# Tokens of experts 2 to 7 gathered as four row pieces and turned by VectorE in 32x32 blocks

## The chip, the cores and the metric

The kernel runs on one core of one Trainium2 chip. The metric is the device time of one execution in microseconds. Before the change it is 1288.38 us, the median of three runs (1286.62 to 1290.02).

## The reference

One transformer layer on 2048 tokens of width 448: layer norm, attention of 16 heads of width 28 that share one key and one value head, output projection and residual, then a second layer norm, a gate over 8 experts, and for each token the two experts with the highest gate values. In fp32:

```python
h = layernorm(x)
p = softmax(causal(q @ k.T * 28 ** -0.5))          # 16 query heads, one k/v head
x1 = x + (p @ v) @ wo
h2 = layernorm(x1)
gate = softmax(h2 @ w_gate)                         # 8 experts
w, idx = top_k(gate, 2)
y = sum(w[e] * (silu(h2 @ w1[e]) @ w2[e]) for e in idx)   # w1: 448x1792, w2: 1792x448
out = x1 + y
```

## The kernel before

The work has four stages on the profile's clock: projections (0 to 84 us), attention (84 to 626), a tail in which the last 512 tokens are normalised, gated and routed while expert 0 already works on two tiles (626 to 690), and the experts (690 to 1290).

**Two-part values.** Every fp32 operand of a product is split in a high and a low part, and a product is three: high by high, high by low, low by high. A token tile (128 tokens) is held transposed, as `xh` (4 blocks of 128 rows) and `xl` (3 blocks). The width of 448 is three and a half blocks; the fourth block holds the last 64 rows' high parts in its upper half and their low parts in its lower half, so the weights' last 64 rows are loaded twice (`load_dup`, L257 to L259, three transfers).

**Tokens on their way to an expert.** In attention, each chunk of 512 tokens ends with its normalised rows and its 8 gate values written to `xnd` in HBM (L407), one row of 456 values a token. Routing makes `il`, a 128 x 128 table of int32: column 16 e + t holds the 128 token rows of tile t of expert e. For a tile, GpSimd gathers 128 rows of `xnd` into one of three buffers (`gather`, L152), TensorE turns them in four transposes through the identity into a bank of PSUM (`transposes`, L242, called by `xprep`, L157), ScalarE writes the high parts (L233, L234), VectorE the low parts (L235, L236), and VectorE copies the expert's gate column (L163).

**An expert.** A run-time Switch on the token counts picks one of the arms written out for an expert: one or two groups of up to four whole tiles and a remainder. `mlp` goes through 14 steps, one for each 128 of the 1792 hidden columns. A step is `first` (11 products of the split w1 with all tokens of the group), ScalarE's two silu outputs (L1021, L1022), VectorE's low part (L1026), and `second` (three products a tile, adding to the tile's output in PSUM). TensorE goes on with the next step's `first` ahead of a step's `second`. At the group's end ScalarE and VectorE scale the outputs and GpSimd adds them into `out` by an indirect scatter (L1097).

**What is woven into the steps.** `hook(k)` runs at each step k. In an expert's first group `ready` prepares the weights of a later step: ScalarE rounds w1 and w2 (L140, L142), VectorE subtracts (L141, L143). `ahead` prepares the tokens that come next: in a last group the first four tiles of the next expert (gathers from step 3, one tile's transposes a step from step 9), before a second group that group's tiles (gathers from step 1, tiles from step 6). Each engine does what it is given in the order written; Switch arms, groups and steps set that order.

Of the kernel before, what the change touches and what calls it, by code (L numbers as in the profile page):

```python
# [37 lines left out]
NF = FF // 128  # L38
OFF = 512
ROW = D + E  # L40
SCALE = DH ** -0.5
BOUND = 30.0
LOOK = 1
# [6 lines left out]
def body(ctx, tc, x, wq, wk, wv, wo, wg, w1, w2, out):  # L50
# [22 lines left out]
    V.memset(ones, 1.0)  # L73

    xnd = dr.tile([OFF + S, ROW], F32, name="xnd")
    ild = dr.tile([128, 128], I32, name="ild")


    il = cst.tile([128, 128], I32, name="il")
# [9 lines left out]
    def const(v, shape):  # L89
# [2 lines left out]
            c = c.unsqueeze(1)  # L92
        return c.to_broadcast(list(shape))

    cw = cst.tile([128, 2 * E], I32, name="cw")
    tok = cst.tile([128, NT], F32, name="tok")
    pcol = cst.tile([128, 1], F32, name="pcol")
# [11 lines left out]
    G.memset(likely, 1)  # L109


    raws, slots, RAW, W = [], [], {}, {}

    def new_slots(pool, n):
        for _ in range(n):
# [41 lines left out]
    def xprep(pt, g, e, x2, i):  # L157
# [4 lines left out]
        weave(split_x(pt[:, :, 0:n], xh[:, :, sl], xl[:, :, sl]))  # L162
        V.tensor_copy(gt[:, i:i + 1], g[:, D + e:D + e + 1])  # L163

    ma = ctx.enter_context(tc.tile_pool(name="ma", bufs=1))
    new_raw(ma)
    new_raw(ma)
    new_slots(ma, 1)
    xa = [new_x(ma, "x0", 4)]
    gbuf = [ma.tile([128, ROW], F32, name=f"g{i}") for i in range(3)]  # L170
    il0 = ma.tile([128, 2], I32, name="il0")


# [77 lines left out]
    def keep_warm(o, n):  # L251

        for _ in range(n):
            mm(o, ident, ident, True, True)

    def load_dup(eng, dst, src):
        eng.dma_start(dst[:, 0:3], src[0:384].rearrange("(k p) n -> p k n", p=128))  # L257
        eng.dma_start(dst[0:64, 3], src[384:448])
        eng.dma_start(dst[64:128, 3], src[384:448])  # L259

    qd = [dr.tile([2, D, 512], F32, name=f"qd{c}") for c in range(NCH)]
    wgd = dr.tile([E, D], F32, name="wgd")
# [50 lines left out]
    def router(c, sm, L, pb, lo=0, n=4, sb4=None, x_out=None, pl=None, oneh=oneh):  # L313
# [381 lines left out]
    with ExitStack() as p2:  # L695
# [35 lines left out]
        def attention(general):  # L731
# [3 lines left out]
            def early(k):  # L735
                if k < 4:
                    V.tensor_copy(wos[k][0], hp3[:, k])
                    G.tensor_tensor(wos[k][1], hp3[:, k], f(wos[k][0]), op=ALU.subtract)
                elif k == 4:
                    pw = psm.tile([128, 512], F32, name="pm")  # L740
                    for k in range(4):
                        n = 128 if k < 3 else 64
                        PE.transpose(pw[0:E, k * 128:k * 128 + n], wgs[0:n, k], ident[0:n, 0:n])
                    V.tensor_copy(lb3[0:E, 0:D], pw[0:E, 0:D])
                    SP.dma_start(wgd[:, :], lb3[0:E, 0:D])
                elif k == 5:
                    SP.dma_start(wgb, wgd[None, :, :].to_broadcast([128, E, D]))
                elif k == 6:
                    for o_, n_ in ((xnd, ROW), (out, D)):
                        SP.dma_start(o_[0:OFF].rearrange("(r p) n -> p r n", p=128),  # L750
                                     xn3[:, 0:1, 0:n_].to_broadcast([128, OFF // 128, n_]))
                else:
                    load(k - 7)

# [241 lines left out]
    with ExitStack() as p3:  # L996
# [234 lines left out]
        def dve(*gens):  # L1231
# [8 lines left out]
                4.5: [(t_tr, 1), (prep, 9)], 4.75: [(prep, 8), (t_tr, 2), (t_gate, 0)],  # L1240
# [3 lines left out]
                8.75: [(prep, 10), dve((g_route, gates), (g_route, put, 1))], 9: [dve((g_route, put, 3)), (prep, 11)], 9.5: [(arms,)],  # L1244
# [30 lines left out]

        def pools(k):
            if k == NF - 1.5:
                rst.close()
                mc = p3.enter_context(tc.tile_pool(name="mc", bufs=1, side="right"))
                xs.append(new_x(mc, "x1", 4))  # L1280
                xb.extend(new_x(mc, "xb", 3.5))
                ybuf.extend(mc.tile([128, D], F32, name=f"y{i}") for i in (2, 3))
                xprep(bank(), gs[0], 0, xb, 0)
# [7 lines left out]
        def tiles(e, lo, n):  # L1291
            return [idx_of(e, lo + t) for t in range(n)]

        def ahead(k, e, lo, n, x2, G1, k0, k1):
# [15 lines left out]
        def run_groups(e, groups, weights, rests=False, begun=False):  # L1310
# [3 lines left out]
            for j, (n, t, x2) in enumerate(groups):  # L1314
# [3 lines left out]
                def hook(k):  # L1318
# [17 lines left out]
                        ready(e * NF + NF + 1)  # L1336
                    if not last:
                        n2, t2, x3 = groups[j + 1]
                        ahead(k, e, lo + n, max(n2 + (t2 > 0), 2), x3, G1, 1, 6)
                    elif e + 1 < E:  # L1340
                        ahead(k, e + 1, 0, 4, xs[(e + 1) % 2], G1, 3, 9)

                add_out(mlp(e, x2, n, t, tiles(e, lo, n + (t > 0)), hook, begun and j == 0))
                lo += n
# [2 lines left out]
        def rest(e, lo):  # L1347

            total = nc.values_load(cw[0:1, e:e + 1], min_val=lo + 1, max_val=16)
            with tc.For_i(lo, total, 2) as ti:  # L1350
                ix = hp.tile([128, 2], I32, name="ix", bufs=1)
                SP.dma_start(ix, ild[:, bass.ds(e * 16 + ti, 2)])
                gather.n = 0
                for i in range(2):
                    xprep(bank(), gather(ix[:, i:i + 1]), e, xb, i)
# [4 lines left out]

        for e in range(E):
            K = KINDS if e else KINDS0
            if e:
                if e + 1 < E:
                    kind.append(kind_of(e + 1))
# [38 lines left out]
_INS = ["A_x", "A_wq", "A_wk", "A_wv", "A_wo", "B_w_gate", "B_w1", "B_w2"]  # L1404


# [17 lines left out]
```

## Time and profile before

| what | value |
|---|---|
| time, median of 3 runs | 1288.38 us |
| the profiled execution: its time | 1292.12 us |
| its span | 1290.2 us |
| TensorE granted clock, mean | 0.99 |
| TensorE busy, projections (0 to 84 us) | 74.99 us |
| TensorE busy, attention (84 to 626) | 541.46 us |
| TensorE busy, tail (626 to 690) | 58.19 us |
| GpSimd gathers L152, count and mean | 42, 1033 ns |
| GpSimd scatters L1097, count and mean | 36, 1599 ns |

How to read it: PE is TensorE's products, PEld its weight loads (they run beside products), DVE is VectorE, ACT ScalarE, POOL GpSimd, SP SyncE, which issues most transfers. A row names the line, the engine, the operation, and output <- input. "x4" is a count of records. A group's row gives its busy time and the mean of one in ns. In brackets on a timeline stands the time that the engine was idle ahead of the row, and what ended it. A windows row has the window, its length, the busy time (and count) of PE, PEld, DVE, ACT and POOL, then the granted clock, the share of the DMA engines and GB/s.

### The profile page before, as it was taken

How to read it: one execution, taken by the hardware profiler on the slowest of the kernel's cores; microseconds unless marked ns; L12 is line 12 of the kernel's file. 1: busy time of each engine (PE TensorE's matmuls, PEld its weight loads, DVE VectorE, ACT ScalarE, POOL GpSimd, SP SyncE). 2: the span in 40 equal slices, each digit the busy share in tenths (PEclk: the TensorE clock that was granted, in tenths of full speed). 3: DMA queues.
4: the chain of work that ended last, by engine and by line, in shares of the span. 5: the costliest groups of instructions: out<-in, count | busy, mean ns of one | idle time of the engine just before them, and what ended most of it. 6: DMA issues, size and time to landing. Idle time of an engine off the chain costs nothing. (4 is left out here: it accounts for less than half of the span.)

```text
span 1290.2 us, 20993 instructions
## 1 busy us (share of the span) xinstructions
PE 1261.6 (98%) x7262; PEld 910.2 (71%) x7262; DVE 598.0 (46%) x1555; ACT 820.4 (64%) x1442; POOL 142.6 (11%) x181
## 2 busy tenths in 40 slices
PE   8999999999999999999999999999999999999996
PEld 7754444554455445545698888998899998898995
DVE  7623222474257723774573445524423454314463
ACT  5689999799988998898642444524423554323453
POOL 5211000000000000000211202102021120112020
PEclk8999999999999999999998999999999999999998
DMA  5732543323232323432363435605341654314462
GB/s 164 214 109 38 152 99 53 66 29 72 41 53 59 67 38 66 95 67 24 93 185 90 118 115 126 188 28 133 92 81 37 167 139 130 79 41 108 128 149 50
DMA packets 81860, 122.12 MB, mean 95 GB/s; under 512 B 10584, under 2 KB 68032, under 8 KB 81528
## 3 DMA queue, kind: packets, MB, share of 16 engines
q1 hardware_dynamic: 71720, 94.99, 30.6%
q0 software_dynamic: 9936, 24.85, 8.7%
q8 instruction: 74, 1.21, 0.4%
q14 instruction: 130, 1.06, 0.3%
HBM read 90.43 MB, written 24.25 MB: 89 GB/s over the span
## 5 line engine op out<-in xcount | busy, mean ns | idle before, releaser
L723 ACT ACTIVATE p<-s 128x1024 f32<-128x1024 f32 x382 | 364.8, 1043 | 0.5 <-issue 0.4
L1021 ACT ACTIVATE s<-p 128x256 f32<-128x256 f32 (+8 forms) x168 | 78.8, 469 | 362.8 <-PE p L62 223.0
L62 PE MATMUL y<-w2h,h 128*128 128x448 f32 (+2 forms) x952 | 281.8, 373 | 0.2 <-DVE h L1026 0.2
L62 PE MATMUL s<-qt,KT 114*128 114x512 f32 x1024 | 277.5, 411 | 1.7 <-ACT p L723 0.7
L62 PEld LDWEIGHTS s<-qt,KT 114*128 114x128 f32 x1024 | 184.6, 188 | 125.7 <-ACT p L723 64.0
L62 PE MATMUL acc<-p,vv 128*32 128x512 f32 x2036 | 245.3, 598 | 0.0
L1026 DVE TENSOR_TENSOR h<-s,h 128x256 fp32r<-128x256 f32 (+5 forms) x168 | 87.6, 521 | 322.7 <-ACT h L1022 306.6
L62 PEld LDWEIGHTS y<-w2h,h 128*128 128x128 f32 (+2 forms) x952 | 170.5, 187 | 18.7 <-DVE h L1026 0.6
L62 PE MATMUL y<-w2l,h 128*128 128x448 f32 (+3 forms) x504 | 177.9, 368 | 0.0
L719 ACT ACTIVATE p<-s 128x512 f32<-128x512 f32 x254 | 138.0, 596 | 48.0 <-PE s L62 39.5
L62 PEld LDWEIGHTS acc<-p,vv 128*32 128x32 f32 x2036 | 53.2, 109 | 106.7 <-issue 105.9
L152 POOL DMA_INDIRECT g<-xnd,il x42 | 43.4, 1033 | 702.5 <-DVE il L872 455.0
L62 PEld LDWEIGHTS y<-w2l,h 128*128 128x128 f32 (+3 forms) x504 | 91.1, 181 | 9.3
L813 DVE RECIPROCAL lb<-lb 128x128 f32<-128x128 f32 x60 | 56.8, 947 | 82.9 <-DMA lb<-o 82.9
L1097 POOL DMA_INDIRECT out<-y,il x36 | 57.6, 1599 | 294.3 <-DVE y L1089 257.9
L1022 ACT ACTIVATE h<-p 128x256 fp32r<-128x256 f32 (+8 forms) x168 | 77.8, 463 | 0.0
L141 DVE TENSOR_TENSOR w1l<-w1r,w1h 128x512 fp32r<-128x512 f32 x109 | 75.1, 689 | 4.1 <-ACT w1h L140 1.2
L140 ACT ACTIVATE w1h<-w1r 128x512 fp32r<-128x512 f32 x112 | 71.0, 634 | 2.2 <-issue 2.2
L143 DVE TENSOR_TENSOR w2l<-w2r,w2h 128x448 fp32r<-128x448 f32 x108 | 66.9, 620 | 0.0
L142 ACT ACTIVATE w2h<-w2r 128x448 fp32r<-128x448 f32 x112 | 64.8, 579 | 0.0
L852 DVE SCALAR_TENSOR_TENSOR junk<-xn,wgb 128x448 f32<-128x448 f32 x96 | 59.6, 621 | 2.6
L62 PE MATMUL p<-x1h,w1h 128*128 128x512 f32 (+2 forms) x224 | 55.3, 368 | 0.5 <-DVE y L1082 0.3
(323 smaller groups left out, 1437.4 us busy)
## 6 DMA issues: line engine op xcount, KB each, us to landing
w2r<-in_B_w SPq DMA_DIRECT2D x56, 448.0 KB
w1r<-in_B_w SPq DMA_DIRECT2D x56, 384.0 KB
qt<-qd SPq DMA_DIRECT2D x64, 224.0 KB
w1r<-in_B_w SPq DMA_DIRECT2D x112, 64.0 KB
qd<-w1r POOLq DMA_DIRECT2D x8, 504.0 KB, 7.2
lb<-o SPq DMA_DIRECT2D x60, 64.0 KB
xnd<-xn SPq DMA_DIRECT2D x4, 912.0 KB
xt<-in_A_x SPq DMA_DIRECT2D x3, 896.0 KB
```

The costliest lines, as they stand in the source:

```text
L62: return PE.matmul(o, a, b, start=start, stop=stop)
L140: A.activation(w[0], a, AF.Copy)
L141: yield eng.tensor_tensor(w[1], a, f(w[0]), op=ALU.subtract)
L142: A.activation(w[2], b, AF.Copy)
L143: yield eng2.tensor_tensor(w[3], b, f(w[2]), op=ALU.subtract)
L719: x = [A.activation(p[:, b], s[:, b], AF.Exp, scale=SCALE) for b in range(2)]
L723: A.activation(p, s, AF.Exp, scale=SCALE)
L852: V.scalar_tensor_tensor(junk, xn[:, 0:D], 1.0, wgb[:, e], op0=ALU.mult, op1=ALU.mult, accum_out=LG[c][:, i, e:e + 1])
L1021: A.activation(s[:, 0:n], p[:, 0:n], AF.Silu)
L1022: A.activation(h[:, 0:n], p[:, 0:n], AF.Silu)
L1026: V.tensor_tensor(h[:, 512:512 + n], s[:, 0:n], f(h[:, 0:n]), op=ALU.subtract)
L1097: d = G.indirect_dma_start(out=out[:, :], out_offset=bass.IndirectOffsetOnAxis(ap=idx, axis=0), in_=y, in_offset=None, compute_op=ALU.add)
```

## The change

For experts 2 to 7 a token is also stored as four rows of `xsd`, each with 128 plain fp32 values (columns 0, 128, 224 and 320 onward) and the 8 gate values. `pieces` and `piece_gates` write them, eight transfers on SyncE's queue behind each chunk's `xnd` (the last chunk's are in the `tail` table at 4.5 and 9.5); rows of zeros are written early, with those of `xnd`.

A tile is gathered by four indirect transfers (`gather4`): in transfer q, partition 32 j + i gets piece j of the tile's token 32 q + i. One VectorE instruction then transposes the tile's 32x32 blocks in place (`turn`); after it a partition holds one column of the tokens. `turned` writes high parts (ScalarE), low parts (VectorE), and forms the gate column by a masked sum over the four 32-partition quarters. The order in which columns come to lie on partitions differs from before, so the host orders the rows of w1 for experts 2 to 7 to suit, and appends the last 64 rows a second time; one transfer loads them in place of three.

`lists4`, at the start of expert 1, makes the lists for the four transfers out of `il`: sixteen products of a 32-column slice of the identity with `il` in fp32 on TensorE, one VectorE instruction (4 x row + piece), and one transfer to HBM. `plan` sets at which step of a group each tile is turned and split; the gathers are all issued from step 1. It counts 5 us of GpSimd for a tile's four gathers. For the arms that the token counts take, the steps (turn, split) are 5,6 6,7 7,8 9,10 in expert 1; 8,9 10,11 12,13 in expert 2's first group; 6,7 7,8 8,9 10,11 in expert 4 (384 columns); 5,6 6,7 7,8 9,10 in expert 6 (448 columns).

```diff
+    xsd = dr.tile([(OFF + S) * 4, SROW], F32, name="xsd")
...
-        load_dup(SP, a, w1[e][:, q * 256:(q + 1) * 256])
+        SP.dma_start(a, w1[e][:, q * 256:(q + 1) * 256].rearrange("(k p) n -> p k n", p=128))
...
+    def gather4(col):
+        st = stage[gather.n % len(stage)]
+        gather.n += 1
+        for q in range(4):
+            G.indirect_dma_start(out=st[:, q], out_offset=None, in_=xsd[:, :],
+                                 in_offset=bass.IndirectOffsetOnAxis(ap=col(q), axis=0))
+        return st
+
+    def turn(st):
+        v = st[:, :, 0:128].rearrange("p i (b r) -> p i b r", r=32)
+        V.transpose(v, v)
+
+    def turned(st, e, x2, i):
+        xh, xl, gt = x2
+        n = min(128, xh.shape[2] - i * 128) // 32
+        v = st[:, 0:n, 0:128].rearrange("p i (b r) -> p b i r", r=32)
+        hi, lo = (t[:, :, i * 128:i * 128 + 32 * n].rearrange("p b (i r) -> p b i r", r=32) for t in (xh, xl))
+        A.activation(hi[:, 0:3], v[:, 1:4], AF.Copy)
+        A.activation(hi[0:64, 3], v[0:64, 0], AF.Copy)
+        V.tensor_tensor(lo, v[:, 1:4], f(hi[:, 0:3]), op=ALU.subtract)
+        V.tensor_tensor(hi[64:128, 3], v[0:64, 0], f(hi[0:64, 3]), op=ALU.subtract)
+        V.scalar_tensor_tensor(own[:, 4:8], st[:, :, 128 + e], 1.0, own[:, 0:4], op0=ALU.mult, op1=ALU.mult,
+                               accum_out=gt[:, i:i + 1])
+
+    def pieces(xn, c):
+        rows = xsd[(OFF + c * 512) * 4:(OFF + c * 512 + 512) * 4].rearrange("(t p j) n -> p t j n", p=128, j=4)
+        for j, o in enumerate(FROM):
+            SP.dma_start(rows[:, :, j, 0:128], xn[:, :, o:o + 128])
...
                 SP.dma_start(xnd[OFF + c * 512:OFF + (c + 1) * 512, :].rearrange("(t p) n -> p t n", p=128), xn)
+                pieces(xn, c)
+                piece_gates(xn, c)
...
+        def lists4():
+            p = bank()
+            for q in range(4):
+                for j in range(4):
+                    mm(p[32 * j:32 * j + 32, q], ident[:, 32 * q:32 * q + 32], ilf, True, True)
+            V.scalar_tensor_tensor(il4[0], p, 4.0, quad[:, None, :].to_broadcast([128, 4, 128]), op0=ALU.mult, op1=ALU.add)
+            SP.dma_start(ild4[:, :, :], il4[0])
...
+            if e > 1:
+                if k == 1:
+                    gather.n = 0
+                    G1.extend(gather4(col4(e, lo + i)) for i in range(min(n, 3)))
+                for i in range(n):
+                    if k == P[i][0]:
+                        turn(G1[i])
+                    if k == P[i][1]:
+                        turned(G1[i], e, x2, i)
+                        if i + 3 < n:
+                            G1.append(gather4(col4(e, lo + i + 3)))
+                return
```

How the order of instructions moves, at two places. On VectorE, in expert 2's first group, a row before is one tile's split between two steps' weights and low parts (`w1l`, `w2l` are the weights' low parts, `h` the hidden layer's, `xbl`, `xbh` and `xbg` the next group's tokens and gates):

```order
L1026 TENSOR_TENSOR h_11932<-s_11930,h_11932 128x256
L1228 ISA x3
L141 TENSOR_TENSOR w1l_11879<-w1r_103,w1h_11878 128x512
L143 TENSOR_TENSOR w2l_11881<-w2r_104,w2h_11880 128x448
L235 TENSOR_TENSOR xbl<-pt,xbh 128x3x128
L236 TENSOR_TENSOR xbh<-pt,xbh 64x128
L163 COPY xbg<-g_114 128x1
L1026 TENSOR_TENSOR h_11933<-s_11931,h_11933 128x256
```

And after, at the first tile's turn (`gb` is the tile that holds all gather buffers):

```order
L1072 TENSOR_TENSOR h_11985<-s_11983,h_11985 128x256
L152 TENSOR_TENSOR w1l_11940<-w1r_118,w1h_11939 128x512
L154 TENSOR_TENSOR w2l_11942<-w2r_119,w2h_11941 128x448
L187 STREAM_TRANSPOSE gb<-gb 128x4x128
L1072 TENSOR_TENSOR h_11986<-s_11984,h_11986 128x256
L152 TENSOR_TENSOR w1l_11944<-w1r_118,w1h_11943 128x512
L154 TENSOR_TENSOR w2l_11946<-w2r_119,w2h_11945 128x448
L197 TENSOR_TENSOR xbl<-gb,xbh 128x3x128
L198 TENSOR_TENSOR xbh<-gb,xbh 64x128
L199 SCALAR_TENSOR_TENSOR own,xbg<-gb,own 128x4
L1072 TENSOR_TENSOR h_11985<-s_11983,h_11985 128x256
```

The turn is a step of its own ahead of the split, which reads `gb` in SBUF where it read PSUM (`pt`), and the gate copy has become a sum. On TensorE, in the same group before, one step's `first`, a tile's transposes, and the start of `second`:

```order
L62 MATMUL p_11928<-x0h,w1h_11870 128x256 x4
L62 MATMUL p_11928<-x0h,w1l_11871 128x256 x4
L62 MATMUL p_11928<-x0l,w1h_11870 128x256 x3
L242 MATMUL pt<-ident,g_114 128x128 x3
L242 MATMUL pt<-ident,g_114 64x128
L62 MATMUL y_39314<-w2h_11868,h_11933 128x448 x2
L62 MATMUL y_39314<-w2l_11869,h_11933 128x448
```

After, the same place:

```order
L64 MATMUL p_11982<-x0h,w1h_11927 128x256 x4
L64 MATMUL p_11982<-x0h,w1l_11928 128x256 x4
L64 MATMUL p_11982<-x0l,w1h_11927 128x256 x3
L64 MATMUL y_38760<-w2h_11925,h_11985 128x448 x2
L64 MATMUL y_38760<-w2l_11926,h_11985 128x448
```

The transposes are gone from the arms of experts 2 to 7 (and from expert 1's, for expert 2's tiles), and nothing stands in their place.

More of the change, by code (lines that the diff above doesn't have):

```diff
@@ L40 @@
 ROW = D + E
+SROW = 128 + E
+FROM = (0, 128, 224, 320)
 SCALE = DH ** -0.5
@@ L75, in body @@
     xnd = dr.tile([OFF + S, ROW], F32, name="xnd")
+    xsd = dr.tile([(OFF + S) * 4, SROW], F32, name="xsd")
     ild = dr.tile([128, 128], I32, name="ild")
+    ild4 = dr.tile([128, 4, 128], I32, name="ild4")
     il = cst.tile([128, 128], I32, name="il")
@@ L93, in const @@
         return c.to_broadcast(list(shape))
+    quad = cst.tile([128, 1], F32, name="quad")
+    own = cst.tile([128, 8], F32, name="own")
+    G.memset(own, 0.0)
+    for j in range(4):
+        G.memset(quad[32 * j:32 * j + 32], float(j))
+        G.memset(own[32 * j:32 * j + 32, j:j + 1], 1.0)
     cw = cst.tile([128, 2 * E], I32, name="cw")
@@ L109, in body @@
     G.memset(likely, 1)
-    raws, slots, RAW, W = [], [], {}, {}
+    raws, slots, RAW, W, il4 = [], [], {}, {}, []
     def new_slots(pool, n):
@@ L163, in xprep, with piece_gates @@
         V.tensor_copy(gt[:, i:i + 1], g[:, D + e:D + e + 1])
+    def gather4(col):
[23 more added lines that the diff above has]
+            SP.dma_start(rows[:, :, j, 0:128], xn[:, :, o:o + 128])
+    def piece_gates(xn, c):
+        rows = xsd[(OFF + c * 512) * 4:(OFF + c * 512 + 512) * 4].rearrange("(t p j) n -> p t j n", p=128, j=4)
+        for j in range(4):
+            SP.dma_start(rows[:, :, j, 128:SROW], xn[:, :, D:ROW])
     ma = ctx.enter_context(tc.tile_pool(name="ma", bufs=1))
@@ L169, in body @@
     xa = [new_x(ma, "x0", 4)]
-    gbuf = [ma.tile([128, ROW], F32, name=f"g{i}") for i in range(3)]
+    gb = ma.tile([128, 12 * SROW], F32, name="gb")
+    gbuf = [gb[:, i * ROW:(i + 1) * ROW] for i in range(3)]
+    stage = [gb[:, i * 4 * SROW:(i + 1) * 4 * SROW].rearrange("p (i n) -> p i n", i=4) for i in range(3)]
     il0 = ma.tile([128, 2], I32, name="il0")
@@ L748, in early @@
                 elif k == 6:
-                    for o_, n_ in ((xnd, ROW), (out, D)):
-                        SP.dma_start(o_[0:OFF].rearrange("(r p) n -> p r n", p=128),
-                                     xn3[:, 0:1, 0:n_].to_broadcast([128, OFF // 128, n_]))
+                    for o_, r_, n_ in ((xnd, OFF, ROW), (out, OFF, D), (xsd, 4 * OFF, SROW)):
+                        SP.dma_start(o_[0:r_].rearrange("(r p) n -> p r n", p=128),
+                                     xn3[:, 0:1, 0:n_].to_broadcast([128, r_ // 128, n_]))
                 else:
@@ L1239, in body @@
                 3.75: [(t_norm, 3, A), (t_norm, 1, A), (t_tr, 0), (t_norm, 2, V), (t_base,)],
-                4.5: [(t_tr, 1), (prep, 9)], 4.75: [(prep, 8), (t_tr, 2), (t_gate, 0)],
+                4.5: [(t_tr, 1), (prep, 9), (pieces, xn3, 3)], 4.75: [(prep, 8), (t_tr, 2), (t_gate, 0)],
                 5: [(t_tr, 3), (t_gate, 1), (t_gate, 2), (t_gate, 3)], 5.5: [(prep, 6)],
@@ L1277, in pools @@
             if k == NF - 1.5:
+                V.tensor_copy(ilf, il)
                 rst.close()
@@ L1280, in pools @@
                 xs.append(new_x(mc, "x1", 4))
+                il4.append(mc.tile([128, 4, 128], I32, name="il4"))
                 xb.extend(new_x(mc, "xb", 3.5))
@@ L1292, in tiles, with col4, plan, ahead @@
             return [idx_of(e, lo + t) for t in range(n)]
-        def ahead(k, e, lo, n, x2, G1, k0, k1):
+        def lists4():
+            p = bank()
+            for q in range(4):
+                for j in range(4):
+                    mm(p[32 * j:32 * j + 32, q], ident[:, 32 * q:32 * q + 32], ilf, True, True)
+            V.scalar_tensor_tensor(il4[0], p, 4.0, quad[:, None, :].to_broadcast([128, 4, 128]), op0=ALU.mult, op1=ALU.add)
+            SP.dma_start(ild4[:, :, :], il4[0])
+        def col4(e, t):
+            return lambda q: il4[0][:, q, e * 16 + t:e * 16 + t + 1]
+        def plan(n, t, m, since):
+            N = n * 128 + t
+            tb = max(N, 256) * 11 * .00046 + (n * 3 + (3 if t > 64 else 2 if t else 0)) * .205
+            pool, P = since * 2.2 + 2, []
+            for i in range(m):
+                k = P[i - 3][1] if i > 2 else 1
+                pool = max(pool, k * tb + 2) + 5
+                P.append([max(-int(-(pool + 4) // tb), P[-1][0] + 1 if P else 0)])
+                P[-1].append(P[-1][0] + 1)
+            over = max(P[-1][1] - NF + 1, 0)
+            return [tuple(max(k - over, 1) for k in p) for p in P]
+        def ahead(k, e, lo, n, x2, G1, k0, k1, P=None):
+            if e > 1:
[10 more added lines that the diff above has]
+                return
             if k == k0:
@@ L1353, in rest @@
                 gather.n = 0
+                if e > 1:
+                    ix4 = hp.tile([128, 4, 2], I32, name="ix4", bufs=1)
+                    SP.dma_start(ix4, ild4[:, :, bass.ds(e * 16 + ti, 2)])
                 for i in range(2):
-                    xprep(bank(), gather(ix[:, i:i + 1]), e, xb, i)
+                    if e > 1:
+                        st = gather4(lambda q: ix4[:, q, i:i + 1])
+                        turn(st)
+                        turned(st, e, xb, i)
+                    else:
+                        xprep(bank(), gather(ix[:, i:i + 1]), e, xb, i)
                 add_out(mlp(e, xb, 2, 0, [ix[:, i:i + 1] for i in range(2)]))
@@ L1362, in body @@
             K = KINDS if e else KINDS0
+            if e == 1:
+                lists4()
             if e:
@@ L1404, with laid_out @@
 _INS = ["A_x", "A_wq", "A_wk", "A_wv", "A_wo", "B_w_gate", "B_w1", "B_w2"]
+def laid_out(inputs):
+    w1 = np.asarray(inputs["B_w1"])
+    tail = [FROM[j % 2] + r for j in range(4) for r in range(32)]
+    rows = [f + 32 * k + r for k in range(3) for f in (32, 160, 256, 352) for r in range(32)] + tail
+    own = list(range(D)) + list(range(384, D))
+    w1 = np.stack([w1[e][own if e < 2 else rows] for e in range(E)])
+    return {**inputs, "B_w1": w1}
 def kernel(**inputs):
```

12 lines of the change are left out of this document (5 added, 7 removed).

## The prediction

> **What bounds the kernel now.** I read the page's busy shares first, then the windows cut at the stages, then TensorE's rows of the experts' stage, one step after another. From the page, the windows, and two views that group rows (all transposes of gathered tiles; VectorE's groups between 690 and 1290 us, where a row is count | busy, mean ns):
>
> ```profile
> PE 1261.6 (98%) x7262; PEld 910.2 (71%) x7262; DVE 598.0 (46%) x1555; ACT 820.4 (64%) x1442; POOL 142.6 (11%) x181
> ...
> 690.00:1290.00 600.00, 586.98 (x3187) 529.84 (x3185) 258.63 (x548) 246.33 (x577) 92.65 (x94) 0.99 0.41 104
> ...
> L242 PE MATMUL pt<-ident,g x156: 270/272/302, 675.1 to 1231.1; 128*128 128x128 f32 x117, 128*64 128x128 f32 x39
> ...
> L235 DVE TENSOR_TENSOR x1l<-pt,x1h 128x384 fp32r<-128x384 f32 x16 | 8.9, 555 | 0.6
> L235 DVE TENSOR_TENSOR x0l<-pt,x0h 128x384 fp32r<-128x384 f32 x12 | 6.7, 556 | 0.0
> L235 DVE TENSOR_TENSOR xbl<-pt,xbh 128x384 fp32r<-128x384 f32 x9 | 5.0, 551 | 0.0
> ```
>
> TensorE is busy 98% of the span and 587.0 of the 600 us in which experts run; VectorE 258.6, ScalarE 246.3, GpSimd 92.7. So the time is what TensorE is given to do, and what leaves TensorE there leaves the time, unless another engine falls behind within a step. The transposes are 156, four a tile, so 39 tiles; 16 + 12 + 9 = 37 of those are finished after 690 us, of which 4 are expert 1's, left as they were. The change takes 33 tiles off TensorE.
>
> **What a tile's transposes cost TensorE.** A step is one 128-column slice of the hidden layer, and its first row is always the x0h by w1h group. Steps in the 448-column, the 384-column and the 256-column groups, TensorE's timeline (start, duration, then the idle time before it in brackets):
>
> ```profile
> 1209.17 0.98 PE L62 MATMUL p<-x0h,w1h 128*128 128x448 f32 x4
> 1213.64 0.99 PE L62 MATMUL p<-x0h,w1h 128*128 128x448 f32 x4
> 1215.91 0.60 PE L242 MATMUL pt<-ident,g 128*128 128x128 f32 x4
> 1218.57 0.98 PE L62 MATMUL p<-x0h,w1h 128*128 128x448 f32 x4
> ...
> 1024.88 0.86 PE L62 MATMUL p<-x0h,w1h 128*128 128x384 f32 x4
> 1028.67 0.86 PE L62 MATMUL p<-x0h,w1h 128*128 128x384 f32 x4
> 1030.61 0.60 PE L242 MATMUL pt<-ident,g 128*128 128x128 f32 x4
> 1032.87 0.86 PE L62 MATMUL p<-x0h,w1h 128*128 128x384 f32 x4
> ...
> 804.95 0.64 PE L62 MATMUL p<-x0h,w1h 128*128 128x256 f32 x4
> 807.50 0.64 PE L62 MATMUL p<-x0h,w1h 128*128 128x256 f32 x4
> 809.84 0.63 PE L242 MATMUL pt<-ident,g 128*128 128x128 f32 x4 [0.86 <-DMA g<-xnd,il]
> 811.52 0.66 PE L62 MATMUL p<-x0h,w1h 128*128 128x256 f32 x4
> 814.52 0.64 PE L62 MATMUL p<-x0h,w1h 128*128 128x256 f32 x4
> ```
>
> Without and with a tile, a step takes 4.47 and 4.93 us (448 columns), 3.79 and 4.20 (384), 2.55 and 3.00 (256, the last two rows): 0.46, 0.41 and 0.45. I take 0.44, not the records' 0.60, which overlap. 33 x 0.44 = 14.5 us. The 0.86 us in which TensorE waits for a gather goes too, since TensorE no longer waits for gathers there: 0.9. Nothing is late next by itself, because the step lengths without a tile are seen in the same group, with the same VectorE and ScalarE work in the steps around.
>
> [...]
>
> **What the change puts on TensorE: the lists.** At the start of expert 1, sixteen products of a 32-column slice of the identity with the list turn it into four lists; an fp32 product shows as two records, so 32 records of 128 columns. Nothing like it is in the trace; nearest are a group with 32-row weights, one-hot bf16 products of 128 columns, and the place where it stands:
>
> ```profile
> 586.16 1.92 PE L62 MATMUL acc<-p,vv 128*32 128x512 f32 x16
> ...
> 666.98 0.69 PE L62 MATMUL y<-y 128*128 128x128 bf16 x8
> ...
> 721.61 0.47 PE L62 MATMUL p<-x1h,w1h 128*128 128x512 f32 x1 [0.35 <-DVE y L1082]
> ```
>
> 32 x 0.12 = 3.8 us by the first (taken: 32-bit, 32 wide), 32 x 0.086 = 2.8 by the second, and as little as 1.4 if 128 columns cost a quarter of 512. TensorE waits 0.35 us for VectorE near there, which the products fill: +3.5, bounds +1.0 to +4.2.
>
> **What it puts on VectorE and ScalarE.** Per tile the 32x32 turn is new; hi copies, lo and tail subtracts remain with another source; the gate copy becomes a masked sum of 4 elements. The tight place is expert 2's first group (2 tiles, 2.55 us a step, weights prepared in each). VectorE's, then ScalarE's groups, by form:
>
> ```profile
> L141 DVE TENSOR_TENSOR w1l<-w1r,w1h 128x512 fp32r<-128x512 f32 x97 | 66.9, 689 | 2.9
> L143 DVE TENSOR_TENSOR w2l<-w2r,w2h 128x448 fp32r<-128x448 f32 x97 | 60.1, 620 | 0.0
> L1026 DVE TENSOR_TENSOR h<-s,h 128x256 fp32r<-128x256 f32 x54 | 23.0, 425 | 84.3 <-ACT h L1022 77.8 <-ACT s L1021 6.6
> ...
> L236 DVE TENSOR_TENSOR x1h<-pt,x1h 64x128 fp32r<-64x128 f32 x16 | 4.6, 284 | 0.5
> ...
> L140 ACT ACTIVATE w1h<-w1r 128x512 fp32r<-128x512 f32 x97 | 61.5, 634 | 0.0
> L142 ACT ACTIVATE w2h<-w2r 128x448 fp32r<-128x448 f32 x97 | 56.1, 579 | 0.0
> ...
> L1021 ACT ACTIVATE s<-p 128x256 f32<-128x256 f32 x26 | 10.0, 385 | 24.4 <-PE p L62 19.3 <-PE y L62 3.7 <-ACT w2h L142 1.4
> ...
> L233 ACT ACTIVATE x1h<-pt 128x384 fp32r<-128x384 f32 x16 | 7.9, 495 | 0.0
> L234 ACT ACTIVATE x1h<-pt 64x128 fp32r<-64x128 f32 x16 | 4.2, 265 | 0.0
> ```
>
> A step with a turn: 0.43 + 0.69 + 0.62 + turn. The turn is not in the trace; it moves 128x512 values, as the 0.69 us group does (taken), bounds 0.55 (128x384) to 1.4 (double): 2.43 us, under 2.55, or 3.1. The step after: 0.43 + 0.69 + 0.62 + 0.555 + 0.284 + the 4-element sum, an estimated 0.15 (half the 64x128 row) = 2.73 on VectorE and 2 x 0.385 + 0.634 + 0.579 + 0.495 + 0.265 = 2.74 on ScalarE, both 0.2 over the step. Three tiles: +0.5, bounds 0 to +2. In steps of 3.79 us and more the same sums fit with about 1 us to spare. The turn waits for its four gathers; behind it on VectorE stand the next weights' lows and h, for which TensorE's second layer waits. That cover is priced under the rivals.
>
> **What it puts on GpSimd.** Four gathers of 128 rows of 544 bytes for one of 1,824: 132 in place of 33. GpSimd's rows, and the issue row with the median time to landing:
>
> ```profile
> 803.00 1.18 POOL L152 DMA_INDIRECT g<-xnd,il  x1 [5.50 <-PE p L62]
> 804.48 0.98 POOL L152 DMA_INDIRECT g<-xnd,il  x1 [0.30 <-issue]
> 805.77 0.95 POOL L152 DMA_INDIRECT g<-xnd,il  x1 [0.30 <-issue]
> ...
> 832.08 1.62 POOL L1097 DMA_INDIRECT out<-y,il  x1 [25.36 <-DVE y L1089]
> ...
> 834.00 1.82 POOL L1097 DMA_INDIRECT out<-y,il  x1 [0.27 <-DMA out<-y,il]
> ...
> g<-xnd,il POOLq DMA_INDIRECT x42, 3.9
> ```
>
> Gathers start 1.29 us apart, with as many rows to describe as the new ones have, so twelve in a row take 15.5 us and the third tile has landed 19.4 us after step 1. Its turn stands at step 12 in expert 2's first group (11 x 2.55 = 28.1 us after step 1), at 8 in the 384-column one (7 x 3.79 = 26.5), at 7 in the 448-column one (6 x 4.47 = 26.8): 7 to 9 us to spare. Cost nothing, hidden behind TensorE's products.
>
> **What it puts on the queues.** In attention each 512-token chunk's normalised rows go out a second time, 1.05 MB in 512-byte packets and four transfers of 32-byte packets, on SyncE's queue behind xnd. SyncE's next transfers there, the window in which the last such xnd write moved, and VectorE's wait for those next transfers:
>
> ```profile
> 589.39 3.20 SPq L803 DMA_DIRECT2D lb<-o  x4
> ...
> 574.00:577.00 3.00, 3.00 (x26) 1.64 (x19) 2.90 (x12) 2.68 (x4) 0.00 (x0) 1.00 0.75 280
> ...
> 598.46 0.95 DVE L813 RECIPROCAL lb<-lb 128x128 f32<-128x128 f32 x1 [9.10 <-DMA lb<-o]
> ```
>
> The xnd write fills 3 us at 280 GB/s; the pieces are about 3.7 us more, to 581, and the queue's next work is issued at 589.4. Hidden, with 8 us to spare. For the last chunk the pieces stand among expert 0's weight loads, where a late load would delay TensorE: 0 to +3, I take +0.3. One weight load in place of three moves the same bytes: nothing.
>
> **Sum.** -14.5 - 0.9 + 3.5 + 0.5 + 0.3 = -11.1 us. The profiled execution took 1292.1 us (span 1290.2), 3.7 above the median of 1288.4; it becomes 1281.0, and the median 1277.3. With every bound on its good side: 33 x 0.46 = 15.2, + 0.9 - 1.0 = 15.1 less, 1273. All on the bad side: 33 x 0.41 = 13.5, - 4.2 - 2 - 3 = 4.3 less, 1284.
>
> **Rivals.** About 0.3%, 3.9 us, is what a measurement here can tell from no change.
>
> *GpSimd sets the pace* (slower). A turn that waits holds up VectorE, then TensorE. It decides where twelve gathers outlast the spare time. With pitch p the third tile is late by 12 x (p - 1.29) - 7 us in each of 9 groups; the gain is used up at 1.2 us a group, p = 1.97. At 2.1 it is 2.7 us a group, 24 in all, 13 over the gain: 1302. For it: the scatters above start 1.92 us apart; the new gathers write smaller rows into one tile; and the new lo subtract reads two SBUF operands while gathers run. Were each gather to wait out one such VectorE instruction (0.69), p would be 1.98, just at the point. Against it: the weights' lows above read two SBUF operands in every step already, and the gathers among them take 0.95 to 1.18. [...] Chance 0.12.
>
> *The written pieces hold up the queue* (about no change). If transfers of small packets ran at a quarter of the rate, about 15 us for 3.7, lb would come 3 us late at 598 and the last chunk's loads 8 us late: +11 in sum, 1288. For it: the 32-byte packets, not seen as writes here; against: the 8 us of room in attention. Chance 0.10.
>
> *The small costs all land on the bad side*: lists 4.2, the tight group +2, the tail +3: 1284, still just faster. It lies in the forecast's own spread; its part over 1284.5 gets 0.04.
>
> **How the numbers follow.** Forecast 0.74 (1273 to 1284), GpSimd 0.12, queue 0.10, small costs 0.04. Leaving out the GpSimd case and the far end of the queue's, the range is 1272 to 1288. Faster (under 1284.5): 0.74 and a little of the queue's, 0.76; same: 0.12; slower: 0.12.
>
> **What would show it.** Right: about 33 fewer groups of four transposes on TensorE, steps of 4.47, 3.79 and 2.55 us throughout, 32 records of some 0.12 us near 721, gathers still 1.3 us apart, a turn near 0.7 us with no wait for its gathers. Wrong: idle time before the turn put down to gathers of xsd, gathers 1.9 us or more apart, TensorE waiting for h after a turn, a wait for lb longer than 9.1 us, or steps of 2.55 grown to 3 in expert 2.

## The result and the profile after

The changed kernel takes 1303.2 us (median of four runs, 1300.2 to 1309.6) against 1288.6 for the kernel before: a ratio of 1.012, 95% interval 1.008 to 1.016. It is slower by about 15 us where 11 us less were forecast. The profiled execution took 1301.95 us, its span 1300.1.

From the page of the changed kernel, its view of VectorE's groups (the turn) and its view of TensorE's waits (total, times, longest):

```profile
PE 1253.7 (96%) x7162; PEld 900.1 (69%) x7162; DVE 618.0 (48%) x1623; ACT 822.1 (63%) x1442; POOL 240.2 (18%) x289
...
L181 POOL DMA_INDIRECT gb<-xsd,il x132 | 130.8, 991 | 124.5 <-issue 85.6
...
L187 DVE STREAM_TRANSPOSE gb<-gb 128x512 f32<-128x512 f32 x33 | 23.3, 705 | 0.5 <-DMA gb<-xsd,il 0.5
...
PE y L64 <- ACT h L1068: 9.6, 5, 5.2
PE y L64 <- ACT s L1067: 4.8, 2, 2.8
...
PE p L64 <- issue: 2.6, 5, 1.0
```

TensorE's records add up to 7.9 us less (1253.7 against 1261.6), yet the span is 9.9 us longer: TensorE is idle for 46.4 us in place of 28.6. The turn, 0.705 us each, waited only 0.5 us in all for its gathers. What TensorE waits for are ScalarE's silu outputs (`s`, `h`) and, oddly, nothing ("issue"), neither of which delayed a second-layer product in the profile of before.

The intended gain is there, step by step. TensorE's timeline of the changed kernel at the same places as shown of before: two ordinary steps of 448 columns in which tiles are now turned, one of 384, and the products that make the lists:

```profile
1225.13 0.96 PE L64 MATMUL p<-x0h,w1h 128*128 128x448 f32 x4
1229.56 0.97 PE L64 MATMUL p<-x0h,w1h 128*128 128x448 f32 x4
1233.99 0.97 PE L64 MATMUL p<-x0h,w1h 128*128 128x448 f32 x4
...
1042.13 0.86 PE L64 MATMUL p<-x0h,w1h 128*128 128x384 f32 x4
1045.86 0.86 PE L64 MATMUL p<-x0h,w1h 128*128 128x384 f32 x4
...
718.01 1.08 PE L64 MATMUL pt<-ilf,ident 128*32 128x128 f32 x32
```

A step with a tile is 4.43 us where it was 4.93, and 3.73 where it was 4.20. The 32 records of the lists take 1.08 us.

The loss stands elsewhere. The same timeline in expert 2's first group, whose steps take 2.51 us:

```profile
801.82 0.63 PE L64 MATMUL p<-x0h,w1h 128*128 128x256 f32 x4
804.33 0.63 PE L64 MATMUL p<-x0h,w1h 128*128 128x256 f32 x4
807.20 0.62 PE L64 MATMUL p<-x0h,w1h 128*128 128x256 f32 x4
813.13 1.06 PE L64 MATMUL p<-x0h,w1h 128*128 128x256 f32 x4
819.04 0.63 PE L64 MATMUL p<-x0h,w1h 128*128 128x256 f32 x4
```

Two steps take 5.9 us each. Such steps stand in six groups, always while gathers run: against the ordinary step of their group they lose 0.7 us in expert 1, 6.8 and 6.9 in expert 2's two groups, 6.9 in expert 3's second, 4.0 in expert 4, 4.1 in expert 5's second, 29 us together. What happens in one is plainest in expert 3's second group. GpSimd's, TensorE's and ScalarE's timelines of the changed kernel there (twelve gathers from 959.23 to 973.08, the first and the last shown):

```profile
959.23 1.04 POOL L181 DMA_INDIRECT gb<-xsd,il  x1 [0.30 <-issue]
960.57 0.98 POOL L181 DMA_INDIRECT gb<-xsd,il  x1 [0.30 <-issue]
...
971.83 0.94 POOL L181 DMA_INDIRECT gb<-xsd,il  x1 [0.30 <-issue]
973.08 0.95 POOL L181 DMA_INDIRECT gb<-xsd,il  x1 [0.30 <-issue]
...
968.11 0.60 PE L64 MATMUL p<-xbl,w1h 128*128 128x320 f32 x3
...
971.37 0.60 PE L64 MATMUL p<-xbl,w1h 128*128 128x320 f32 x3
977.19 1.20 PE L64 MATMUL y<-w2h,h 128*128 128x448 f32 x2 [5.22 <-ACT h L1068]
...
962.30 0.44 ACT L1067 ACTIVATE s<-p 128x320 f32<-128x320 f32 x1 [2.49 <-issue]
...
976.37 0.44 ACT L1067 ACTIVATE s<-p 128x320 f32<-128x320 f32 x1 [9.21 <-issue]
...
977.02 0.45 ACT L1067 ACTIVATE s<-p 128x320 f32<-128x320 f32 x1
```

TensorE ends two steps' first-layer products at 968.71 and 971.97. ScalarE, free since 967.15, starts their silus at 976.37 and 977.02: 7.7 and 5.1 us late, where 0.04 to 0.1 us is usual. Its wait at that point is for semaphores of VectorE and TensorE; VectorE's last work was done at 967.74. The trace's record of semaphore updates (the signals by which one engine tells another that work is done) settles which: after two at 971.34 and 971.38 a single one of TensorE's arrives, at 973.51, then eleven within 0.42 us from 976.30 on, some 3 us after the last gather began. The products behind those of 968.11 start at their usual distances, so the work was done and the news of it was late. I call the time from the end of a step's first-layer products to ScalarE's start the lag. Before, it is over 1 us in two steps of 138 after 725 us (1.06 at 807.5, in the only group whose three gathers meet steps this short, and 1.3 at the last scatters); after, in 17, at most 8.1. ScalarE's news is not late: VectorE, when it is free, starts on ScalarE's `h` 0.03 us after it as a rule and 0.09 at most, with gathers running or not.

Twelve gathers do not always cost time. In the longest steps (4.96 us: the first groups of experts 3 and 5) the lags are 0.7 and 2.8 us and TensorE loses nothing; in expert 6's group the first nine gathers stand 1.6 to 1.8 us apart, and the lag stays at 0.1.

The same backlog shows on TensorE itself, which stands still between products that have no wait (TensorE's timeline, expert 2's second group, gathers running since 837.6):

```profile
851.77 0.39 PE L64 MATMUL p<-xbl,w1h 128*128 128x288 f32 x1 [0.21 <-issue]
853.19 0.29 PE L64 MATMUL p<-xbl,w1h 128*128 128x288 f32 x1 [1.03 <-issue]
853.92 0.40 PE L64 MATMUL p<-xbl,w1h 128*128 128x288 f32 x1 [0.44 <-issue]
855.73 0.74 PE L64 MATMUL y<-w2h,h 128*128 128x448 f32 x1 [1.41 <-ACT h L1068]
```

A part of the loss is not idle time. Behind four of these stops TensorE's granted clock is half of full. Windows of the changed kernel, in and behind a stop of expert 2's second group, then of expert 3's:

```profile
849.90:853.90 4.00, 2.35 (x14) 1.86 (x12) 0.00 (x0) 0.00 (x0) 1.89 (x2) 0.99 0.20 52
853.90:860.70 6.80, 5.38 (x17) 4.23 (x17) 2.57 (x9) 2.04 (x6) 1.13 (x2) 0.50 0.00 1
...
972.70:976.70 4.00, 0.00 (x0) 0.00 (x0) 0.00 (x0) 0.33 (x1) 1.02 (x2) 1.00 0.13 35
976.70:980.10 3.40, 2.91 (x8) 2.37 (x9) 1.12 (x4) 1.09 (x4) 0.00 (x0) 0.51 0.00 0
```

With two more such stretches, at 812.9 and 1157.6, these are 17.1 us between 690 us and the last 10 us of the span, where the kernel before has none. The records stretch accordingly: two products of 0.57 us as a rule take 1.20 at 977.19.

### The profile page after: what moved, and what is told of

Same layout as the page of the kernel before. It is cut to its first block, busy times and chain, and to the rows that moved or that the text cites. A ratio compares the mean times of both kernels' runs of the same rounds, so it can differ in the third digit from the quotient of the medians.

```text
span 1300.1 us, 20906 instructions
## 1 busy us (share of the span) xinstructions
PE 1253.7 (96%) x7162; PEld 900.1 (69%) x7162; DVE 618.0 (48%) x1623; ACT 822.1 (63%) x1442; POOL 240.2 (18%) x289
## 3 DMA queue, kind: packets, MB, share of 16 engines
q14 instruction: 130, 1.06, 0.3%
## 5 line engine op out<-in xcount | busy, mean ns | idle before, releaser
L181 POOL DMA_INDIRECT gb<-xsd,il x132 | 130.8, 991 | 124.5 <-issue 85.6
L163 POOL DMA_INDIRECT gb<-xnd,il x9 | 9.9, 1098 | 502.3 <-DVE il L918 454.6
```

The lines of the kernel that those rows point to most:

```text
L181: G.indirect_dma_start(out=st[:, q], out_offset=None, in_=xsd[:, :], in_offset=bass.IndirectOffsetOnAxis(ap=col(q), axis=0))
```

## The experiments

The theory (A): gathers issued by GpSimd one right behind the other delay TensorE's semaphore updates; ScalarE starts late, then VectorE, then TensorE's second layer. The rivals (B): the new VectorE and ScalarE work, or the bytes of the gathers, hold up the steps; later, that GpSimd's being busy or the mere arrival of many small transfers does it.

| run | edit | median, us | ratio to before, 95% |
|---|---|---|---|
| e1_spaced | one small memset ahead of each gather | 1305.1 | 1.009 to 1.019 |
| e2_paced | gathers issued at later steps | 1303.6 | 1.008 to 1.015 |
| e3_before_extra | before, with three more gathers behind each | 1318.9 | 1.019 to 1.028 |
| e4_tiny | rows of 32 bytes | 1305.0 | 1.009 to 1.015 |
| e5_pool_work | iota in place of gathers | 1274.3 | 0.986 to 0.990 |
| e6_sp | SyncE's transfers in place of gathers | 1272.0 | 0.985 to 0.988 |
| e7_pitch | two longer memsets ahead of each gather | 1302.7 | 1.007 to 1.011 |
| e8_bursts | 4.7 us of memsets behind every four | 1294.8 | 1.003 to 1.005 |
| e9_bursts_planned | 2.3 us, and turns planned for it | 1276.2 | 0.988 to 0.991 |
| e10_short_planned | 1.2 us, and turns planned for it | 1276.6 | 0.989 to 0.992 |
| e11_plan_only | e9 without its memsets | 1316.1 | 1.019 to 1.023 |
| e12_half_rows | gathers of 64 rows | 1317.1 | 1.019 to 1.024 |

**e1_spaced.**

```diff
         for q in range(4):
+            G.memset(spacer, 0.0)
             G.indirect_dma_start(out=st[:, q], ...
```

> The changed kernel with one small GpSimd memset ahead of each of the four gathers, as the scatters have one between them; nothing else. Theory A: a run of gathers started 1.25 us apart delays TensorE's semaphore updates, ScalarE starts its silu up to 8 us late and TensorE stands still, 29 us in all. With a pitch of about 1.9 us the lag from the end of a step's first-layer products to ScalarE's start stays under 0.3 us, and the time falls from 1303 to about 1274; up to 1282 if the third tile, landed 12 x 1.9 + 4 = 27 us after step 1, comes too late for its turn in some groups. Theory B (the new VectorE and ScalarE work, or the bytes of the gathers, hold up the steps): 1300 to 1306, as the changed kernel.

1305.1 us, but the edit didn't do what it was meant to. Between the scatters the same memset takes 0.63 us; here 0.088, inside the 0.3 us that lie between gathers anyway, and the gathers stayed 1.25 us apart for the most part. The lags stayed too (up to 7.5 us). It tells nothing between the theories.

**e2_paced.**

```diff
...
-                if k == 1:
-                    gather.n = 0
-                    G1.extend(gather4(col4(e, lo + i)) for i in range(min(n, 3)))
+                for i in range(min(n, 3)):
+                    if k == P[i][2]:
+                        G1.append(gather4(col4(e, lo + i)))
```

> The changed kernel with the first three tiles' gathers issued not all at step 1 but two or three steps apart (at least 7.5 us from tile to tile where the group is long enough), turns planned after that; pitch within a tile's four gathers still 1.25 us. Theory A, if a backlog builds up only over a long run: lags under 0.3 us, 1274 us, range 1271 to 1280. If the pitch itself does it, four in a row also delay: a lag of about a microsecond a tile, 1285 or so. Theory B: 1300 to 1306.

1303.6 us, and again no pace: nothing ties a gather to a step. GpSimd goes on to the next gather whatever stands beside it in the program; the trace shows the same runs of twelve, 1.25 us apart for the most part, and lags up to 6.7 us. The edit paced nothing, so this too tells nothing between the theories.

**e3_before_extra.**

```diff
+        if more4:
+            for q in range(3):
+                G.indirect_dma_start(out=dump[(gather.n * 3 + q) % 5], out_offset=None, in_=xnd[:, :].rearrange("a b -> (a b)")[0:rows * 136].rearrange("(r n) -> r n", n=136),
+                                     in_offset=bass.IndirectOffsetOnAxis(ap=idx, axis=0))
         return g
...
```

> The kernel before, with three more gathers of 128 rows of 544 bytes behind each gather for experts 2 to 7, into buffers that nobody reads; TensorE still transposes. Theory A: the gathers alone bring the lags, TensorE loses 20 to 30 us, 1309 to 1320 (a few us of it waits of the transposes for gathers that now land later). Theory B: the extra gathers are hidden, 1287 to 1292.

1318.9 us, 30 us more than before. From its page (the 99 added gathers) and its view of TensorE's waits:

```profile
L156 POOL DMA_INDIRECT dump<-xnd,il x99 | 97.0, 980 | 31.7 <-issue 31.4
...
PE y L62 <- ACT h L1027: 17.0, 6, 5.5
PE pt L247 <- issue: 2.0, 2, 1.0
```

Nobody reads what these gathers bring, nothing else was changed, and the waits for ScalarE's `h` appear, with lags up to 10.8 us. That the new VectorE work is needed for the loss is out. The gathers alone cost 30 us, as much as the 29 us counted in the changed kernel.

**e4_tiny.**

```diff
-            G.indirect_dma_start(out=st[:, q], out_offset=None, in_=xsd[:, :],
+            G.indirect_dma_start(out=st[:, q, 128:SROW], out_offset=None, in_=xsd[:, :].rearrange("a b -> (a b)")[0:(OFF + S) * 4 * 8].rearrange("(r n) -> r n", n=8),
...
```

> The changed kernel with rows of 32 bytes in place of 544 in each gather (the tiles' 128 values are not brought, so the experts work on other data); as many gathers and rows as before. Theory A, with the number of row descriptors and not the bytes as the cause: lags as in the changed kernel, 1298 to 1306. If the bytes or the traffic are the cause: lags gone, 1272 to 1280.

1305.0 us: a seventeenth of the bytes, the same loss. Not the bytes.

**e5_pool_work.**

```diff
-            G.indirect_dma_start(out=st[:, q], out_offset=None, in_=xsd[:, :],
-                                 in_offset=bass.IndirectOffsetOnAxis(ap=col(q), axis=0))
+            for _ in range(3):
+                G.iota(st[:, q], pattern=[[1, SROW]], base=0, channel_multiplier=0, ...)
```

> The changed kernel with every one of the 132 gathers of experts 2 to 7 replaced by three iota instructions of GpSimd that write the same 136 columns (so these experts work on counted numbers): GpSimd is busy for as long, but describes no transfers. If describing or completing gathers delays TensorE's updates: no lag over 0.3 us but for the few in expert 0's stage, 1272 to 1278. If GpSimd's being busy (its port, its instructions) is the cause: lags as in the changed kernel, 1298 to 1306.

1274.3 us. GpSimd was busy for less than meant (396 iotas of 0.25 us are 94 us, against 131 of gathers), but after 725 us there is no lag over 0.9 us, and those over 0.3 stand at scatters. In e9_bursts_planned GpSimd is busy for 307 us in all (240 in the changed kernel), and the lag is gone as well. Being busy is not it.

**e6_sp.**

```diff
-            G.indirect_dma_start(out=st[:, q], out_offset=None, in_=xsd[:, :],
-                                 in_offset=bass.IndirectOffsetOnAxis(ap=col(q), axis=0))
+            SP.dma_start(st[:, q], xsd[OFF * 4 + q * 128:OFF * 4 + q * 128 + 128])
```

> The changed kernel with each gather replaced by a plain transfer of 128 rows of 544 bytes from the same table, issued by SyncE (so the tiles hold other tokens): as many transfers, rows, bytes and completions, described by hardware and not by GpSimd. If GpSimd's describing is the cause: no lags, 1272 to 1280 (a little more where a weight load stands behind a fourth tile's transfers on SyncE). If arrival and completion of many small transfers is the cause: lags as before, 1298 to 1306.

1272.0 us, 17 us under before. As many transfers with as many bytes, issued by SyncE and closer together (twelve in 7.8 us in expert 2's first group), and after 725 us no lag over 0.4 us but at scatters (1.7 at most). From its page and its view of VectorE's groups:

```profile
PE 1243.6 (98%) x7162; PEld 896.1 (71%) x7162; DVE 618.7 (49%) x1623; ACT 822.9 (65%) x1442; POOL 108.6 (9%) x157
...
L186 DVE STREAM_TRANSPOSE gb<-gb 128x512 f32<-128x512 f32 x33 | 23.3, 705 | 0.0
```

GpSimd has 132 records fewer than in the changed kernel (157 for 289). TensorE is back at 98% and 10.1 us less busy with the same products, and a turn that never waits hides wholly. This is what the change is worth without the lag, and the lag needs GpSimd's gathers.

**e7_pitch.**

```diff
         for q in range(4):
+            G.memset(wide, 0.0)
+            G.memset(wide, 0.0)
             G.indirect_dma_start(out=st[:, q], ...
```

> The changed kernel with two memsets of 300 values ahead of each gather, meant to set the gathers some 1.9 us apart (the 1-value memset of the earlier run took 0.09 us and left the pitch at 1.25). If the rate is the cause, as the stretch of expert 6 suggests, where gathers 1.6 to 1.8 us apart showed lags of 0.1 us: lags under 0.3 us, 1274, up to 1284 if third tiles land too late for their turns. If any long run of gathers is the cause, whatever its rate: 1300 to 1310.

1302.7 us, for another reason than the changed kernel. The gathers now stand 1.85 to 3.8 us apart, and ScalarE's `h` is gone from TensorE's waits. In its place, in VectorE's groups, TensorE's waits and ScalarE's timeline:

```profile
L190 DVE STREAM_TRANSPOSE gb<-gb 128x512 f32<-128x512 f32 x33 | 23.4, 709 | 66.6 <-DMA gb<-xsd,il 66.5
...
PE y L64 <- DVE h L1075: 20.9, 13, 3.7
...
826.40 0.52 ACT L198 ACTIVATE xbh<-gb 128x384 fp32r<-128x384 f32 x1 [4.36 <-DVE gb L190]
827.03 0.36 ACT L1070 ACTIVATE s<-p 128x256 f32<-128x256 f32 x1
```

The turns wait 66.5 us for gathers that come later, and VectorE's `h` behind them: the wait that was the prediction's GpSimd rival, here made by the cure. The longest lag left, 4.2 us, is ScalarE's own copy in front of the silu, which waits for a turn. The time lies in the range that was expected if any long run of gathers does the harm, but by accident. The trace's record of TensorE's updates settles the question: each of the 872 that add one after 725 us arrives within 0.22 us of the end of its product. So runs of up to sixteen gathers, 1.85 us or more apart, delay no update: it is the pitch that matters.

**e8_bursts.**

```diff
             G.indirect_dma_start(out=st[:, q], ...
...
+        for _ in range(12):
+            G.memset(wide, 0.0)
         return st
```

> The changed kernel with twelve memsets of 300 values behind each tile's four gathers, about 4 us of other GpSimd work between bursts of four gathers 1.25 us apart. If the backlog of TensorE's updates needs a run of more than four or five: lags under 0.5 us, 1274 to 1282. If it is the pitch within a burst: lags of 1 to 3 us remain, 1282 to 1300.

1294.8 us, in the range that was expected if the pitch within a burst did it, but again the rows show another cause. Four gathers 1.25 us apart and then a pause bring no lag of their own (all 872 such updates arrive within 0.02 us); the longest that is left, 3.9 us at 871, is ScalarE's copy behind a turn. The rest is the turn (46.7 us of waiting for gathers) and TensorE's 12.9 us for VectorE's `h`.

**e9_bursts_planned.**

```diff
+        for _ in range(6):
+            G.memset(wide, 0.0)
         return st
...
                 P[-1].append(P[-1][0] + 1)
-            over = max(P[-1][1] - NF + 1, 0)
-            return [tuple(max(k - over, 1) for k in p) for p in P]
+                pool += 2.5
+            last = [min(p[0], NF - 1 - m + i) for i, p in enumerate(P)]
+            return [(k, k + 1) for k in last]
```

> The changed kernel with six memsets of 300 values (some 2.4 us) behind each tile's four gathers, and turns planned for 7.5 us a tile in place of 5, none shifted earlier than its tile needs. In the run with twelve memsets ScalarE's lag was gone, but turns waited 46.7 us in sum for gathers that came later. If both are cured: ScalarE's lag under 0.5 us, turns waiting under 10 us in sum, 1276, range 1272 to 1283, so faster than the kernel before (1289). If 2.4 us between bursts is too short for the backlog: lags of 2 us and more return, 1285 to 1300.

1276.2 us, 12.6 under the 1288.8 of the kernel before in the same comparison. In every step that ends while gathers run, ScalarE starts within 0.1 us, and the turns wait 0.5 us in all: both waits are cured. (Two lags over 0.5 us are left, against what was expected, 2.3 us at 726 and 1.5 at 1229.5; both stand at scatters, with no gather of the split rows near.) Its timelines of GpSimd and ScalarE in expert 3's second group, and its groups of VectorE and waits of TensorE:

```profile
952.37 0.94 POOL L182 DMA_INDIRECT gb<-xsd,il  x1 [0.30 <-issue]
953.30 2.32 POOL L185 MEMSET wide<- 1x300 f32 x6
955.99 0.95 POOL L182 DMA_INDIRECT gb<-xsd,il  x1 [0.37 <-ACT h L1071]
...
958.05 0.44 ACT L1070 ACTIVATE s<-p 128x320 f32<-128x320 f32 x1 [2.46 <-issue]
...
961.30 0.44 ACT L1070 ACTIVATE s<-p 128x320 f32<-128x320 f32 x1 [2.49 <-issue]
...
L190 DVE STREAM_TRANSPOSE gb<-gb 128x512 f32<-128x512 f32 x33 | 23.3, 705 | 0.5 <-DMA gb<-xsd,il 0.3
...
PE y L64 <- DVE h L1075: 1.1, 2, 0.9
```

ScalarE comes every 3.25 us, as the 320-column steps do, through all the gathers.

**e10_short_planned.**

```diff
-        for _ in range(6):
+        for _ in range(3):
...
-                pool += 2.5
+                pool += 1.3
```

> The same with three memsets (some 1.2 us) behind each tile's four gathers and 6.3 us a tile in the plan. If a short pause lets TensorE's updates catch up: 1274 to 1282, as the run with six. If the mean rate of gathers decides (four in 6.3 us against four in 7.5 and twelve in 15): lags between those of the changed kernel and those of the longer pause, 1280 to 1295.

1276.6 us. A gap of 2.44 us in place of 1.25 from every fourth gather to the next is enough, though sixteen gathers then run within 23 us in expert 2's second group.

**e11_plan_only.**

```diff
-        for _ in range(6):
-            G.memset(wide, 0.0)
         return st
```

> The run with six memsets, its later turns kept and the memsets taken out. If the pause between bursts did it: lags of several microseconds are back and the time is 1295 to 1306, as the changed kernel. If the later turns did it: 1273 to 1280.

1316.1 us, above the range that was expected, with lags up to 10 us. So the pause cures the lag and the later turns do not. Why it is 13 us slower than the changed kernel is only known in part: its runs of gathers are the same length, but in its profile TensorE is idle for 57.6 us (46.4 in the changed kernel) and has the half clock for 41 us before the last stretch (17.1).

**e12_half_rows.**

```diff
-            G.indirect_dma_start(out=st[:, q], ...ap=col(q), axis=0))
+            G.indirect_dma_start(out=st[0:64, q], ...ap=col(q)[0:64], axis=0))
```

> The changed kernel with gathers of 64 rows in place of 128 (the other half of each tile stays zero, so the experts work on other data); as many gathers, no pause. If the number of rows described in a stretch loads the path of TensorE's updates: lags roughly halved or gone, 1272 to 1288. If each gather counts alike, whatever its rows, and they now start closer together: lags as in the changed kernel or worse, 1298 to 1312.

1317.1 us, above both ranges. The gathers' row, and TensorE's waits in this run:

```profile
L181 POOL DMA_INDIRECT gb<-xsd,il x132 | 124.3, 942 | 136.7 <-issue 108.4
...
PE y L64 <- ACT h L1069: 12.7, 4, 5.3
PE y L64 <- issue: 12.4, 4, 6.3
```

Half the rows take GpSimd 942 ns where 128 take 991, so the gathers come 1.21 us apart, and the lag is not cured. That it is worse need not be the closer pitch: e11_plan_only came as high with whole rows. What brings the lag is the gather, not the row or the byte.

## Why the prediction was wrong

**Right: what bounds the kernel and what a tile is worth.** The steps with a tile shrank by 0.50 us (448 columns) and 0.47 (384), where 0.46 and 0.41 were read; 33 tiles are some 15.5 us where 14.5 were summed. The wait for a gather at 810 went too. Ordinary steps got 0.04 to 0.07 us shorter as well (4.47 to 4.43, 3.79 to 3.73, 2.55 to 2.51), which nothing in the prediction foresaw and which I can't explain; with it e6_sp gained 17 us where 11 were forecast.

**Right, and over-priced: the lists and the tight group.** The lists cost 1.08 us of records and about 0.3 us of time (the two steps around them take 7.21 us in place of 6.88) where +3.5 was taken: the row chosen as nearest, 0.12 us a record, was three and a half times the 0.034 measured. A record of 128 columns cost about a quarter of one of 512, as the lowest bound had it; but a quarter of 0.12 makes 0.96 us for 32, not the 1.4 that the prediction writes. Expert 2's first group, when nothing else delays it, runs at 2.51 us a step with tiles in it, so +0.5 was nothing. The turn at 0.705 us is the 0.69 that was taken.

**Right: the queues.** In attention nothing moved (541.27 us of TensorE in 542, before 541.46); the wait of 2.4 us for a gather at 680 us is 1.2 in the changed kernel, which is not its doing: e3_before_extra, which has none of it there, gains as much.

**The step that failed: "Cost nothing, hidden behind TensorE's products."** It asked only when a gather lands and who needs its data. By that measure it was right: the turn waited 0.5 us in all, at a pitch of 1.25 us for the most part. It put the price of 99 more gathers at nothing and didn't ask what GpSimd's work does to engines that don't use its data. "Nothing is late next by itself" failed with it: TensorE's semaphore updates were late. What it cost can be read from e6_sp, the same work without the lag. From expert 1's first step to the end, its profile is 20.3 us shorter than before, and that of the changed kernel 31.4 us longer than e6_sp's: +11 together. Over the whole span these two differ by 29.9 us, of which 19.8 are TensorE's idle time and 10.1 longer records; half of the 17.1 us at half clock, an estimated 8.5, is most of these.

**The rivals.** The one on the slow side named the right engine and the wrong mechanism: the pitch was 1.25 us for the most part, far from its threshold of 1.97, the turns hardly waited, and a run of gathers close together, not far apart, did the harm. That its 1302 us lies beside the measured 1303 is chance. Its wait did come true in e7_pitch and e8_bursts. Its other leg, VectorE instructions with two SBUF inputs that hold up the gathers, was a supposition that no run shows: the new lo subtract takes 0.55 us, as the one from PSUM did, and the gathers 0.99 on average, where those of before took 1.03.

**What was there to be read.** The trace of before had two signs. One is that no more than three gathers ever stood in a row at 1.3 us; the scatters, which come up to four in a row, stand 1.9 us apart with a memset of 0.63 us between them. The other is ScalarE's timeline of the kernel before in expert 2's first group, after three gathers:

```profile
803.91 0.39 ACT L1021 ACTIVATE s<-p 128x256 f32<-128x256 f32 x1 [0.90 <-PE p L62]
...
807.49 0.39 ACT L1021 ACTIVATE s<-p 128x256 f32<-128x256 f32 x1 [1.94 <-PE y L62]
...
809.03 0.38 ACT L1021 ACTIVATE s<-p 128x256 f32<-128x256 f32 x1
```

The silus should come every 2.55 us; the one at 807.49 comes 3.58 after the last, 1.06 us after its products ended, and TensorE just bridged it. A run of twelve lay outside what the rows showed, so "nothing" should have had a bound of its own for the other engines, not just for the turn.

**What stays open.** Why GpSimd's gathers delay TensorE's updates was not found. e4, e5, e6 and e12 leave neither bytes, rows, GpSimd's work nor completions as such, and e9 and e10 show that a short pause keeps it away. Whether TensorE is hit and ScalarE not because it posts the most updates (1548 with 2816 products after 725 us, against some 550 each of VectorE and ScalarE) was not tried. Nor was the part of the recording: each time on record comes with a recorded span and clock, and in the changed kernel 274 of the 6054 updates of these three engines are missing from the trace, in e5 to e10 none. So records go missing where the lag is, and that the delay is as long with nothing recorded is not shown.

## What to carry to other kernels

Moving work off the full engine was worth at least what the steps without it showed, but a count that is multiplied on an idle engine (33 gathers to 132) needs a price for the others too: look for the longest run of that instruction that the trace has already survived, and treat anything longer as unpriced. When an engine starts late with its input done and "issue" as the reason, compare the producer's end with the consumer's start; a lag that grew over a run of GpSimd's gathers was late semaphores here (7.7 us at 976.37), and a pause of 1.2 us after every four cured it (e10_short_planned, 1276.6 us), provided that the consumers were planned for the later landing. A long stop cost twice here: as idle time (5.22 us ahead of 977.19), and by a clock of 0.51 for the 3.4 us behind it. A gather's place in the program paced nothing (e2_paced: still 1.25 us apart for the most part), and a memset of 0.088 us in the gap of 0.3 between gathers did not either (e1_spaced); longer work on the same engine did (e7_pitch: 1.85 us or more).

## What the runs showed of the hardware

- Twelve gathers 1.25 us apart delayed TensorE's semaphore updates by up to 8 us in the changed kernel; it began at the fifth in expert 2's first group (1.6 us) and the sixth in expert 3's second (0.9). Four at that pitch with 2.44 us to the next four (e10_short_planned) show no lag over 0.1 us while gathers run. Runs of up to sixteen gathers 1.85 us or more apart (e7_pitch) delayed none: 0.22 us at most. ScalarE's updates to VectorE were not late (0.03 us).
- Four times in the changed kernel the granted clock was 0.50 to 0.51 for 3.4 to 6.8 us behind 4 us in which TensorE had stood idle for 1.7 to 4.0. After 1.8 idle of the 4 us up to 819 it was 1.00 (819 to 823).
- A gather of 128 rows took GpSimd 0.94 us (median) with 544 bytes a row (the changed kernel) and with 32 (e4_tiny), one of 64 rows 0.91 (e12_half_rows).
- A 32x32 block transpose of 128x512 fp32 values took VectorE 0.705 us (mean of 33), and TensorE's 32-column fp32 products of 128 columns 0.034 us a record (32 in 1.08).
